# An early activation-table load, five key-weight transfers and a new engine order in a fused attention and gated-MLP kernel

## The chip, the cores and the metric

The kernel runs on one core of one Trainium2 chip. The metric is device time in microseconds (us) of one execution; lower is better. A core has engines that each run their own list of instructions in order and wait for each other by semaphores: TensorE (PE in the profile, with PEld for its weight loads), VectorE (DVE), ScalarE (ACT), GpSimd (POOL) and SyncE (SP). Transfers are issued from SP and ACT and move on 16 DMA engines. Matmul results land in PSUM, everything else lives in SBUF.

## The reference

One transformer block on 2048 tokens of width 640, in bf16. The first half is linear attention with 32 heads of 20 channels, where queries and keys go through a learned feature map (two softmaxes over 20 channels); the second is a bilinear gated MLP of width 1536.

```python
def _A_ref(x, wqkv, w_phi, wo):
    B, S, D = x.shape
    H = 32; Dh = D // H
    q, k, v = ...                                   # x @ wqkv, split in heads
    pq = jnp.einsum("bhsd,hdf->bhsf", q, w_phi)
    pk = jnp.einsum("bhsd,hdf->bhsf", k, w_phi)
    phi_q = concat([softmax(pq), softmax(-pq)], -1)
    phi_k = concat([softmax(pk), softmax(-pk)], -1)
    kv = jnp.einsum("bhsf,bhsd->bhfd", phi_k, v)
    z  = jnp.einsum("bhsf->bhf", phi_k)
    num = jnp.einsum("bhqf,bhfd->bhqd", phi_q, kv)
    den = jnp.einsum("bhqf,bhf->bhq", phi_q, z)[..., None] + 1e-6
    return (num / den).transpose(0, 2, 1, 3).reshape(B, S, D) @ wo

h  = x + _A_ref(_layernorm(x), wqkv, w_phi, wo)
hn = _layernorm(h)
h2 = h + ((hn @ w_gate) * (hn @ w_up)) @ w_down
```

## The kernel before

The 2048 tokens are 16 tiles of 128, the width 640 is 5 chunks of 128. The feature weights are folded into the projections: the product of the key columns of wqkv with a block-diagonal matrix Phi (built from w_phi) is formed once on TensorE, and the same for the queries, so that keys and queries each need one projection per tile. Layer norm is folded in as well: the weights are centred by their column means, and each tile's scale rs multiplies inside the exponential.

**The start.** The steps that the change touches, in the order in which they depend on each other:

- `load_wnat(1, ...)` (L491) brings the key columns of wqkv into Wnat, in chunks of 128 rows (160 KB each). Wnat, and the transposed WT, lie in the memory of the tile phiqT, so the profile calls both phiqT. Before, there are three transfers: chunks 0 and 1 from SP, 2 and 3 from ACT, 4 from SP. w_phi goes into Wrows from ACT, between them. Then SP issues transposing loads of x (`load_xT`, tile xT) and the value columns (tile Wp, 800 KB).
- `warm(32)` (L563) runs 32 matmuls of 128 columns on a constant tile `ones` while the first transfer is under way.
- `wk_in` (L630) takes the key chunks in the order WKC: for each chunk, 5 one-column matmuls for the means and 5 transposes (L639). When the last chunk's means are there, VectorE writes `nmean` (L651). Then the transposed weights are centred and copied out of PSUM in five pieces: pieces 0 and 2 on ScalarE (L658), 1, 3 and 4 on VectorE (L662).
- `wp_round(1, i)` (units x0 to x4, L678) multiplies those pieces with Phi: x0 in three steps (pieces 0 and 1, 2 and 3, then 4), every other round in one step that needs all five. Phi is built on POOL in five pieces (L542). The results are copied into Wp by ScalarE (x0, x2, x4) and VectorE (x1, x3).
- `stats` (units s0, s2, s4, s8, s12, L570) finds mean and scale of 2 or 4 tiles: matmuls on TensorE, copies and sums on VectorE (sm L599, t L604, sxx L607), small operations on POOL (msq L610, vpe, rs L617, nrs L619, mv L621).
- `wv_sums` (unit wv, L711) and `wv_centre` (units c0 to c4, L725) centre the value weights.
- `keys(t)` (units k and K): projection, maximum (L755), bias nb (L758), two exponentials on ScalarE (L762), sums (L773) and reciprocal on VectorE, a product on POOL (L776). `values(t)` (v), `queries(t)` (q and Q, whose results are transposed by DMA into phiqT), `kv_mm` (A0 to A14), `num(t)` (n), `watt(t)` (h: output projection and residual; its result is transposed into hT), `fu` (f, gate and up products) and `fd` (d, e: down product and output) follow.

**The order.** ORDER (L58) is a table with a list of units for each engine: each word stands for the next operation of that unit on that engine. `Prog.place` (L199) walks the lists and assigns buffers; `finish` derives the semaphore waits. So an engine never runs an operation ahead of one that stands before it in its list, and SP issues its transfers in the order of its list: lT4 to lT15 are x transposes, lwq the query columns, t0 to t4 their transposed form, lx0 to lx3 the rows of x for the residual, lwo, lg, lu and ld the weights wo, w_gate, w_up and w_down. PSUM is four buffers (`p_ps`) of two banks. w_down takes the place of the values (tile vaug), so `ld` waits for the last kv_mm.

Of the kernel before, what the change touches and what calls it, by code (L numbers as in the profile page):

```python
# [7 lines left out]
ACT = mybir.ActivationFunctionType  # L8
# [39 lines left out]
WKC = (0, 1, 4, 2, 3)  # L48
# [24 lines left out]
    "DVE":  # L73
# [11 lines left out]
    "ACT":  # L85
# [290 lines left out]
def _build(ctx, nc, A_x, A_wqkv, A_w_phi, A_wo, B_w_gate, B_w_up, B_w_down, out):  # L376
# [5 lines left out]
    def regs(n):  # L382
        return [Reg() for _ in range(n)]
# [669 lines left out]
```

## Time and profile before

| what | value |
|---|---|
| runs | 283.45 us median of 3 (283.38 to 283.68) |
| profiled execution | 283.33 us, of which the span of its instructions is 281.6 us |
| PE busy | 274.1 us, 97% of the span |
| DVE, ACT, POOL busy | 165.9, 133.0, 108.2 us |
| granted TensorE clock | 1.00 over the span |
| chain that ended last, by engine | PE 92%, DVE 3%, ACT 2%, DMA 1%, issue 1% |
| DMA | 28.06 MB, mean 100 GB/s |

Transfers from issue to landing, median us: a 640 KB load of x 5.1, w_up 11.5, w_gate 8.3, w_down 9.3, value columns 5.1; key columns, SP 320 KB 3.9, ACT 320 KB 4.2, SP 160 KB 4.3; w_phi (25 KB) 4.5; a transpose of queries (160 KB) 2.5.

How to read it: an engine's busy time is the union of its instructions' times. The granted clock in the profile starts at its first record, 5.07 us into the span; before that, matmuls of 128 columns start 107 ns apart, and 55 ns after. The chain of waits goes back from the last instruction: at each step to what released it, or to the instruction ahead of it on its engine. A row of the timeline has start, length, engine, line, operation, tiles (out<-in) and count, and in brackets how long the engine had been idle and what ended that.

### The profile page before, as it was taken

The page shows a single profiled execution, that of the slowest core. Times are in us where ns is not written, and L with a number is a line of the kernel's source. Part 1 is how long each engine was busy: PE and PEld are TensorE (multiplying, and loading weights), DVE is VectorE, ACT ScalarE, POOL GpSimd, SP SyncE. Part 2 cuts the span into 40 slices and gives each one's busy share as a digit, 9 for nine tenths or more (in the row PEclk, how much of TensorE's full clock was granted, in tenths as well). Part 3 has the DMA queues.
Part 4 walks back from the last instruction along what each step waited for, and adds up shares of the span by engine and source line. Part 5 has one row for each costly group of instructions (what it writes and reads, how often), then busy time and mean ns, then how long its engine had stood idle before and what let it go on. Part 6 is the DMA issues. An engine that isn't in the chain of part 4 may idle for free.

```text
span 281.6 us, 5487 instructions
## 1 busy us (share of the span) xinstructions
PE 274.1 (97%) x2238; PEld 187.0 (66%) x2251; DVE 165.9 (59%) x289; ACT 133.0 (47%) x225; POOL 108.2 (38%) x160
## 2 busy tenths in 40 slices
PE   8799999999999999999999999999999999999995
PEld 7577778777867888877666554776554444447773
DVE  0699999999989987737756763621402233240211
ACT  0648999799655645226653622023344233330141
POOL 6636889999722522020350354012050051000341
PEclk9999999999999999999999999999999999999999
DMA  7958894018742869925626448164320001000111
GB/s 191 210 120 243 159 262 158 0 38 261 181 85 47 103 137 205 282 48 117 49 48 166 69 94 136 29 140 27 70 72 0 0 0 49 0 0 2 51 72 64
DMA packets 65192, 28.06 MB, mean 100 GB/s; under 512 B 55696, under 2 KB 63888, under 8 KB 65168
## 3 DMA queue, kind: packets, MB, share of 16 engines
q1 hardware_dynamic: 64240, 27.37, 44.2%
q10 hardware_dynamic: 928, 0.35, 0.5%
q8 instruction: 17, 0.28, 0.5%
q14 instruction: 7, 0.06, 0.1%
HBM read 11.82 MB, written 2.62 MB: 51 GB/s over the span
## 4 chain that ended last, share of the span: by engine, by line
PE 92%; DVE 3%; ACT 2%; DMA 1%; issue 1%; POOL 0%; ACTq 0%
PE ps L559 91%; DMA phiqT<-in_A_wqkv_dram 1%; ACT phik L762 1%; DVE ob L874 1%; DVE Wp L725 1%; ACT phiqT L658 1%; ACT L658 0%; DVE phik L916 0%; PE ps L639 0%; PE ps L481 0%; DVE ps L755 0%; DVE outb L957 0%; ACT phik L484 0%; DVE rden L873 0%; DVE Sq L795 0%
## 5 line engine op out<-in xcount | busy, mean ns | idle before, releaser
L559 PE MATMUL ps<-phik,Wgu 128*128 128x512 bf16 (+1 forms) x588 | 105.6, 336 | 0.7
L559 PEld LDWEIGHTS ps<-phik,Wgu 128*128 128x128 bf16 x600 | 58.1, 98 | 43.6 <-DVE phik L916 1.1
L559 PE MATMUL ps<-Wp,xT 128*128 128x320 bf16 x480 | 68.8, 299 | 0.1
L916 DVE TENSOR_TENSOR phik<-ps,gate 128x512 bf16<-128x512 f32 (+1 forms) x60 | 34.0, 580 | 58.1 <-PE ps L559 37.2
L914 ACT ACTIVATE gate<-ps 128x512 bf16<-128x512 f32 (+1 forms) x60 | 29.8, 511 | 74.2 <-PE ps L559 62.7
L559 PE MATMUL ps<-vaug,phik 128*128 128x320 bf16 (+3 forms) x543 | 60.0, 270 | 0.1
L559 PEld LDWEIGHTS ps<-Wp,xT 128*128 128x128 bf16 x480 | 46.2, 98 | 17.9 <-ACT phik L762 0.5
L559 PEld LDWEIGHTS ps<-vaug,phik 128*128 128x128 bf16 x544 | 43.6, 97 | 16.0
L776 POOL TENSOR_TENSOR phik<-phik,Rk 128x1280 bf16<-128x1280 bf16 x16 | 37.5, 2356 | 1.9 <-DVE nb L758 1.4
L932 POOL TENSOR_TENSOR outb<-t,x_all 128x640 bf16<-128x640 f32 x12 | 16.7, 1397 | 54.2 <-ACT t L929 54.1
L801 POOL TENSOR_TENSOR rq<-Sq,rq 128x32 f32<-128x32 f32 x16 | 4.1, 253 | 60.5 <-DVE rq L800 60.5
L755 DVE TENSOR_REDUCE ps<-ps 128x1 f32<-128x640 f32 x32 | 25.8, 812 | 2.3 <-PE ps L559 2.2
L929 ACT ACTIVATE t<-ps,mh,rs 128x640 f32<-128x640 f32 x12 | 10.5, 882 | 34.1 <-PE ps L559 34.1
L795 DVE TENSOR_REDUCE Sq<-eq 128x64 f32<-128x1280 bf16 x16 | 23.6, 1476 | 3.4 <-ACT eq L762 3.3
L773 DVE TENSOR_REDUCE Ssum<-phik 128x64 f32<-128x1280 bf16 x16 | 23.6, 1473 | 0.0
L806 POOL TENSOR_TENSOR eq<-eq,rq 128x640 bf16<-128x640 bf16 x16 | 20.3, 1269 | 1.0
L762 ACT ACTIVATE eq<-ps,nb,rs 128x640 bf16<-128x640 f32 x16 | 14.1, 881 | 8.8 <-DVE nb L758 8.2
L899 POOL TENSOR_SCALAR vpe<-shc 128x1 f32<-128x1 f32 x16 | 3.0, 190 | 38.6 <-ACT junk L552 37.7
L552 ACT ACTIVATE junk<-x_all 128x640 bf16<-128x640 bf16 x20 | 14.8, 741 | 4.9 <-DVE x_all L893 4.9
L762 ACT ACTIVATE phik<-ps,nb,rs 128x640 bf16<-128x640 f32 x16 | 14.3, 893 | 4.0 <-POOL nrs L619 3.3
L782 ACT ACTIVATE vaug<-ps,rs 128x640 bf16<-128x640 f32 x16 | 12.9, 804 | 3.9 <-PE ps L559 3.6
L874 DVE TENSOR_TENSOR ob<-ps,rden 128x640 bf16<-128x640 f32 x16 | 13.0, 814 | 2.4 <-DMA vaug<-ob 2.1
(79 smaller groups left out, 237.1 us busy)
## 6 DMA issues: line engine op xcount, KB each, us to landing
x_all<-in_A_x_dram SPq DMA_DIRECT2D x4, 640.0 KB, 5.1
out_dram<-outb SPq DMA_DIRECT2D x15, 160.0 KB, 1.9
Wgu<-in_B_w_up_dram SPq DMA_DIRECT2D x1, 1920.0 KB, 11.5
Wgu<-in_B_w_gate_dram SPq DMA_DIRECT2D x1, 1920.0 KB, 8.3
vaug<-in_B_w_down_dram SPq DMA_DIRECT2D x1, 1920.0 KB, 9.3
Wp<-in_A_wqkv_dram SPq DMA_DIRECT2D x1, 800.0 KB, 5.1
phiqT<-in_A_wqkv_dram SPq DMA_DIRECT2D x1, 800.0 KB, 6.5
Wo<-in_A_wo_dram SPq DMA_DIRECT2D x1, 800.0 KB, 5.4
```

The source lines that it names most:

```text
L552: g.op("ACT", lambda e: e.activation(out=junk[:, v.i, :], in_=in_, func=func, accum_out=acc), rd=rd, wr=wr, use=[v], t=0.73, lat=0.97)
L559: ins = e.matmul(o_, lhsT=l_, rhs=r_, start=s_, stop=p_, skip_group_check=True)
L755: g.op("DVE", lambda e: e.tensor_reduce(out=mx(), in_=PS[v.i][:, :, 0:HALF], axis=AX.XY, op=ALU.max, apply_absolute_value=True, negate=Tru ...
L762: g.op("ACT", lambda e, s=s, sc=sc: e.activation(out=signed(dst(), s), in_=PS[v.i][:, :, 0:HALF].rearrange("p b (h f) -> p b h f", f=DH), ...
L773: g.op("DVE", lambda e: e.tensor_reduce(out=Ssum[:, vs.i, :], in_=x, axis=AX.X, op=ALU.add), rd=R_phik[t], wr=vs.R, use=[vs], t=1.39, lat=1.5)
L776: g.op("POOL", lambda e: e.tensor_tensor(out=x, in0=x, in1=Rk[:, vr.i, :].unsqueeze(2).to_broadcast([P, 2 * H, DH]), op=ALU.mult), rd=vr.R ...
L795: g.op("DVE", lambda e: e.tensor_reduce(out=Sq[:, vs.i, :], in_=eq[:, b.i, :].rearrange("p (g f) -> p g f", f=DH), axis=AX.X, op=ALU.add), ...
L806: return e.tensor_tensor(out=x, in0=x, in1=rq[:, vr.i, :].unsqueeze(2).to_broadcast([P, H, DH]), op=ALU.mult)
L874: g.op("DVE", lambda e: e.tensor_tensor(out=ob[:, vo.i, :].rearrange("p (b h d) -> p b h d", b=2, d=DH), in0=pv()[:, :, :, 0:DH], in1=rd_( ...
L914: g.op("ACT", lambda e: e.activation(out=gate[:, vg.i, 0:P * n], in_=PS[v.i][:, 0, 0:P * n], func=ACT.Copy), rd=[v.R[0]], wr=vg.R, use=[v, ...
L916: g.op("DVE", lambda e: e.tensor_tensor(out=hhT[:, hb, ft, sl], in0=PS[v.i][:, 1, 0:P * n], in1=gate[:, vg.i, 0:P * n], op=ALU.mult), rd=[ ...
L932: g.op("POOL", lambda e: e.tensor_tensor(out=outb[:, vo.i, :], in0=t32[:, v3.i, :], in1=x_all[:, t, :], op=ALU.add), rd=v3.R + [R_h[t]], w ...
```

## The change

- **Key weights.** Five transfers of one chunk each: SP issues chunks 0, 1 and 3, ACT issues 2 and 4. w_phi is the first transfer of the ACT queue. WKC becomes 0, 1, 2, 3, 4.
- **Table load.** Behind these transfers ScalarE runs an Exp of one column into the scratch tile `junk`, with `ones` as its input. The value columns are then issued from ACT, behind it, where SP issued them before.
- **Phi.** Each of its five pieces has a dependency of its own; the x and y rounds wait for the pieces that they use. (All rounds but x0 use all five.)
- **Warm-up.** 26 matmuls in place of 32.
- **Order.** All five lists of ORDER are new. At the start, x3 and x2 stand ahead of the statistics of s0; POOL's nrs of s0 stands ahead of s2's first operation. On SP, lx2, lx1 and lx0 stand between the first query transposes, lg behind them, and ld directly behind n2's transpose (before: behind Q4's). The planner's figure for a load's rate is 0.38 in place of 0.35; it enters only the choice of buffers and semaphores in `place`.

```diff
-WKC = (0, 1, 4, 2, 3)
+WKC = (0, 1, 2, 3, 4)
...
     "PE":
-        "warm wk wk wk wk wk wk wk wk wk wk s0 x0 s0 x0 x0 x3 x2 x1 x4 wv k0 k0 k0 k0 k0 s2 s2 k1 k3 k2 s4 s4 s4 s4 v3 v1 "
...
+        "warm wk wk wk wk wk wk wk wk wk wk x0 x3 x0 x2 s0 s0 x0 x1 x4 wv k0 k0 k0 k0 k0 s2 s2 k1 k3 k2 v0 s4 s4 s4 s4 k4 "
...
+        "v12 k12 k14 v5 k13 A0 A2 A4 A6 A0 A2 A4 v14 q2 A6 A8 v13 q3 A10 q6 A8 v15 A10 A12 A12 A12 A14 A14 q5 n1 n0 q7 n1 n0 "
+        "n2 h1 h0 h1 q4 n3 h0 h2 f0.7.0 f0.7.0 f0.9.0 f0.9.0 f0.10.0 f0.10.0 f0.11.0 f0.11.0 f0.8.0 f0.8.0 h3 f0.6.0 q8 "
...
     "DVE":
-        "wk wk wk wk s0 s0 x3 s0 x1 c2 c4 k0 s2 s2 k0 c3 s2 k1 c1 k1 c0 k3 k2 s4 s4 k2 s4 k3 K0 s4 K1 K0 k6 K3 k6 k7 K3 "
...
+        "wk wk wk wk x3 s0 s0 s0 x1 c4 c0 k0 s2 s2 k0 c2 k1 c3 k1 c1 s2 k3 k2 K0 s4 k2 s4 s4 k3 s4 k4 K0 K2 k4 K1 k5 K1 "
...
     "ACT":
-        "in in wk wk x0 x4 x2 k0 k0 k1 k1 v3 k3 v1 k3 k2 v7 k2 k6 k6 k7 k7 k5 k5 v2 s12 k4 wm k4 k11 v6 k11 y2 v9 k10 k10 "
...
+        "in in in in in wk wk x2 x0 x4 k0 k0 k1 k1 v0 k2 k2 k3 v2 k3 k4 v3 k4 k5 k5 k7 k7 k6 k6 s12 v9 k10 v10 k10 v7 k9 "
...
     "SP":
-        "in in in in in in in lT6 lT5 lT4 lT7 t1 lT11 lT9 t0 lT8 lT10 lx3 lwq t4 lT14 t2 t3 lT13 lT12 lwo lT15 lu Q0 Q1 "
-        "Q1 lg Q0 lx0 Q2 Q2 Q3 Q3 n2 n3 Q5 Q5 Q7 Q7 h3 h2 Q6 Q6 lx1 n5 n7 Q4 Q4 ld n6 n4 Q8 h7 h6 h4 Q8 Q9 h5 Q9 Q10 Q10 "
...
+        "in in in in in in in lT4 lT6 lT7 lT5 lT8 lT12 lx3 lT9 lT11 lT10 t3 lwq t2 t0 t4 lT14 t1 lwo lT13 lT15 lu Q1 lx2 "
+        "Q1 lx1 Q0 lx0 Q0 lg Q2 Q2 Q3 Q3 n2 ld n3 Q5 Q5 h2 Q7 Q7 h3 Q6 Q6 Q4 n7 Q4 n5 n4 n6 Q8 Q8 Q10 h5 h7 Q10 h4 Q9 h6 "
...
-    load_wnat(1, (0, 2))
-    load_wnat(1, (2, 4), "ACT")
     load(Wrows[:, :, :], A_w_phi.rearrange("h d f -> (h d) f").rearrange("(a p) f -> p a f", p=P), [R_Wrows], 0.03, eng="ACT")
-    load_wnat(1, (4, 5))
-    load_xT(0)
-    load_xT(1)
-    load(Wp[:, :, 2 * D:3 * D], A_wqkv[:, 2 * D:3 * D].rearrange("(c p) n -> p c n", p=P), R_Wp[2], 0.8)
-    load_xT(2)
-    load_xT(3)
+    load_wnat(1, (0, 1))
+    load_wnat(1, (2, 3), "ACT")
+    load_wnat(1, (1, 2))
+    load_wnat(1, (4, 5), "ACT")
+    load_wnat(1, (3, 4))
+    for t in range(4):
+        load_xT(t)
...
+    g.op("ACT", lambda e: e.activation(out=junk[:, 0, 0:1], in_=ones[:, 0:1], func=ACT.Exp), rd=[R_one], wr=[R_tab], t=1.4)
+    load(Wp[:, :, 2 * D:3 * D], A_wqkv[:, 2 * D:3 * D].rearrange("(c p) n -> p c n", p=P), R_Wp[2], 0.8, eng="ACT")
...
-        pool_op(phi_op, 0.4, rd=[R_Wrows, R_G[a]], app=[R_Phi])
+        pool_op(phi_op, 0.4, rd=[R_Wrows, R_G[a]], wr=[R_Phi[a]])
...
-    warm(32)
+    warm(26)
```

More of the change, by code (lines that the diff above doesn't have):

```diff
@@ L448, in _build @@
     R_xT, R_phik, R_vaug = regs(NT), [regs(2) for _ in range(NT)], regs(NT)
-    R_Wnat, R_WT, R_Phi = regs(NC), [regs(NC) for _ in range(2)], Reg()
+    R_Wnat, R_WT, R_Phi = regs(NC), [regs(NC) for _ in range(2)], regs(NC)
     R_Wp = [regs(NC) for _ in range(3)]
@@ L457, in _build @@
     R_mx, R_nb = regs(2 * NT), regs(2 * NT)
-    R_const, R_xone = Reg(), Reg()
+    R_const, R_xone, R_tab = Reg(), Reg(), Reg()
     R_KV, R_Gk = Reg(), Reg()
@@ L463, in load @@
     def load(out_, in_, wr, mb, after=(), eng="SP", app=()):
-        return g.op(eng, lambda e: e.dma_start(out_, in_), wr=wr, app=app, after=after, dma=("w", 8), t=0.6, lat=0.4, size=mb / 0.35)
+        return g.op(eng, lambda e: e.dma_start(out_, in_), wr=wr, app=app, after=after, dma=("w", 8), t=0.6, lat=0.4, size=mb / 0.38)
     def transpose(out_, in_, rd, wr, use=(), t=1.27, size=1.07):
@@ L700, in wp_round @@
             n = len(aa) * (2 - w)
-            g.op("PE", lambda e, lst=lst: mms(e, lst()), rd=[R_WT[w][a] for a in aa] + [R_Phi] + ([R_nmu] if w == 0 else []),
+            g.op("PE", lambda e, lst=lst: mms(e, lst()), rd=[R_WT[w][a] for a in aa] + [R_Phi[a] for a in aa] + ([R_nmu] if w == 0 else []),
                  wr=v.R, use=[v], t=0.062 * n, lat=0.15 + 0.062 * n)
```

73 rows, old and new, of the table ORDER are left out of this document.

## The prediction

> **What bounds the kernel.** I read the page's shares first, then the busy time by stage, then the chain of waits over the first 45 us, and last the order of instructions over the first 16 us. The stages (stretch, length, busy time of PE, PEld, DVE, ACT, POOL):
>
> ```profile
> 0.00:5.00 5.00, 3.83 (x39) 3.58 (x40) 0.00 (x0) 0.00 (x0) 3.54 (x24) 1.00 0.62 169
> 5.00:10.00 5.00, 3.05 (x64) 2.70 (x61) 1.85 (x6) 2.76 (x3) 3.13 (x7) 1.00 1.16 289
> ...
> 20.00:40.00 20.00, 20.00 (x195) 15.21 (x193) 19.67 (x36) 17.10 (x25) 14.72 (x19) 1.00 0.90 204
> 40.00:60.00 20.00, 20.00 (x195) 15.24 (x194) 19.37 (x28) 18.56 (x31) 19.37 (x17) 1.00 0.28 101
> 60.00:80.00 20.00, 20.00 (x279) 16.30 (x278) 18.71 (x33) 15.59 (x29) 16.39 (x12) 1.00 0.62 174
> 80.00:100.00 20.00, 19.34 (x187) 15.26 (x185) 18.69 (x37) 12.53 (x23) 5.48 (x9) 1.00 0.52 79
> ```
>
> From 20 us on TensorE has work without a break; the largest hole is 0.66 us in 80 to 100. None of that work is removed. So the change can win where TensorE waits, before 20 us, or lose by tearing a hole later. VectorE is nearly as full (76.4 of 80 us from 20 to 100), so a hole there costs too. The start, as the chain of waits has it (start, length, what):
>
> ```profile
> 0.79 3.92 DMA phiqT<-in_A_wqkv_dram
> ...
> 4.76 0.30 PE ps L559 x5
> 5.05 0.36 PE ps L639 x5
> 5.41 0.10 PE ps L559 x5
> 5.51 0.30 PE ps L639 x5
> ...
> 6.78 0.18 DVE nmean L651
> ...
> 7.03 1.28 ACT L658
> 8.32 1.49 ACT phiqT L658 x2
> 9.81 0.05 issue
> 9.85 1.65 PE ps L559 x28
> 11.51 0.04 issue
> 11.55 1.53 PE ps L559 x10
> 13.08 0.02 issue
> 13.10 1.55 DVE Wp L725 x2
> ...
> 15.80 0.24 POOL nrs L619
> ```
>
> The reader is to see a strictly serial start: key weights land (4.71), five steps of means and transposes, nmean, then on ScalarE a 1.28 us piece with no tile name, which the order of instructions names:
>
> ```profile
> 1.04 3.59 PE L559 MATMUL ps<-ones 128*128 128x128 bf16 x32 [1.04 <-POOL ones L517]
> 5.91 1.97 POOL L542 TENSOR_TENSOR Phi<-Wrows,G 128x140 bf16<-128x140 bf16 x5 [1.33 <-DMA Wrows<-in_A_w_phi_dram]
> 7.03 1.28 ACT L658 ACT_TABLE_LOAD   x1 [7.03 <-DVE nmean L651]
> 7.08 1.47 DVE L662 TENSOR_SCALAR phiqT<-ps,nmean 128x640 bf16<-128x640 bf16 x3
> ```
>
> **The sum**, against the profiled execution's 283.33 us (span 281.6 and 1.73 around it); the median of the runs, 283.45, is 0.12 higher.
>
> *(a) Key weights and warm-up.* A warm-up matmul costs 0.104 us (3.33 us of weight loads over 32), so 26 end at 1.04 + 2.71, some 3.8, in place of 4.4. Chunk 0 alone (160 KB) is now first on SP, issued at 0.79. No row has a lone 160 KB load from memory at the start: the quick bound is the queries' 160 KB transposes, 2.5 us from issue to landing (3.3), the slow one the 160 KB key chunk that was third in line, 4.3 (5.1). I take 3.0, since it is half of the 320 KB transfer that took 3.92 with nothing ahead: 3.8, just when the warm-up ends. The first step costs 0.65 (0.30 and 0.36 at the slow clock) and the later ones 0.40. Two slow steps, two fast and the last means (0.12): 3.8 + 1.30 + 0.80 + 0.12, and nmean starts at some 6.1 to 6.2, against 6.78. A chunk 0 as late as 4.3 gives the same, because the clock has risen by its second step. The other chunks must keep up. SP issues 1 and 3 at 1.3 and 1.8; ACT issues w_phi, 2 and 4 at 0.8, 1.35 and 1.9 (0.48 to 0.52 each). All key data had landed by 5.60 before; as many bytes on the same engines give 5.3 to 6.3, where the upper end is 4.4 after the last issue. Taken 5.7, under the 6.0 at which chunk 4 has its turn. Term: -0.65, bounds -0.95 and +0.35 (chunk 0 at 5.1 and all five steps after it).
>
> *(b) Table load.* The load (1.28) and a 1-column activation (0.19, the row of L734) now run on ScalarE from 2.4 to 3.9, inside its idle time up to 7.03: cost nothing there. From nmean's start to the last centred piece took 3.03 (6.78 to 9.81); without the load VectorE's three pieces end 1.77 after it (8.55) and ScalarE's two 1.74 (0.25 + 1.49). Term: -1.26. The value weights queue behind it on ACT: issued at 3.9, landed at 9.0 by the 5.09 us that this transfer took before, needed at 10.2. The cover is 1.2 us; a transfer of over 6.3 us would show.
>
> *(c) Order of the start.* The two statistics groups of s0 (0.28 each) filled the wait before; now they stand behind x3 and x2, which need all five pieces, so they lie on the path: +0.57. PSUM has four buffers and each x round finds one free in this order. The value sums then start at 11.55 - 0.65 - 1.26 + 0.57 = 10.2.
>
> *(d) nrs.* POOL's negated scale of s0 stood behind s2's first operation and came at 16.03, when the key bias was ready at 15.85; now it stands ahead of it. Term -0.1 (bounds -0.2 and 0).
>
> w_phi first and one dependency per Phi piece: VectorE and ScalarE have all pieces at 7.9; even a w_phi landing as late as before gives Phi at 7.88. Nothing; if Phi came later, x3 would wait for it one for one.
>
> *(e) The rest of the order.* On SP the value load (0.58) leaves and a third key chunk (0.45) comes, so the x transposes start 0.5 later and end as before; the last of the four that s8 needs should land at 25, needed at 27; the last query weight transpose at 34 to 35, needed near 40. x_all 1 and 2 and w_gate move to 58 to 66 us, and 3.8 MB at the rate of w_gate's 1.9 MB in 8.3 us are in by 76, before the next query transposes (75.9 before). w_down moves from 108 to just behind n2's transpose, at 84.6 - 1.35 = 83.3, and n3's transpose is queued behind it: w_down landed after 9.26, so 92.6, and the transpose 0.6 later (the trace's gap at 117.4 to 118.0): 93.2, against h3's turn at 94.40 - 1.35 = 93.05. Taken +0.1 for all. Bounds: -0.66 (the hole of 80 to 100 closed) and +2.4 (w_down as slow as w_up, below).
>
> Sum: -0.65 - 1.26 + 0.57 - 0.1 + 0.1 = -1.34, so 282.0 us.
>
> By the Trainium skill (DMA: Bandwidth & Descriptors, "Issuing engines are not separate DMA queues") all queues share the same 16 engines and a second one saves only issue time. The rows lean that way: four first transfers of 25 to 320 KB took 3.9 to 4.5 us whatever their size; by the rule (a) is near nothing and the time is the first rival's.
>
> **The rivals.**
> *Splitting brings nothing (0.20).* The 1.1 us from the issue to the first packet in the trace and a slow first flow set the landing, and chunk 0 comes at 4.7. For it: 25 KB took 4.5 us, 320 KB 3.9. Against it: the 25 KB and the 160 KB stood behind others. nmean at 6.78, the other terms stay: 283.33 - 0.69 = 282.6.
> *The gain is lost behind the start, or the table is loaded twice (0.11).* VectorE at 96% from 20 to 100 lets a worse fit of order give back 1.2 us, or the early Exp brings a table set that Identity does not find, and 1.28 comes back at the old place. Against the latter: one load serves Identity, Exp, Square and Copy in the whole trace. About 283.2.
> *w_down too early (0.11), slower.* If w_down takes the 11.5 us of w_up (same size) and not 9.26, n3's transpose lands at 83.3 + 11.5 + 0.6 = 95.4 and TensorE, in order, stands before h3 for 2.35 us: 282.0 - 0.1 + 2.35 = 284.2. It turns the sign from a landing of 94.5 on. For it: transposes share those engines in that stretch; against it: w_up stood behind w_o and a transpose, w_gate took 8.3.
> *The clock stays low (0.08), slower.* The 32 warm-ups ran at 107 ns apart, the transposes at 55 only from 5.1 on. With 26 and gaps between landings TensorE may stay slow to the value sums: steps of 0.65 put nmean at 6.75, and 2.2 us of x rounds and statistics double: 282.0 + 0.6 + 2.2 = 284.8. It turns the sign when the slow clock lasts beyond some 10 us (0.6 and 0.75 of doubled work). Against it: the gaps are short.
> The Trainium skill (TensorE: Matmul & The Clock Gate, Part 1) counts some 3.4 us of sustained work in a free-running window; 26 warm-ups are 2.7 us, so by it the matmuls behind them have to fill in. The trace agrees on about 4 us before the rise (1.04 to 5.1).
>
> **How the numbers follow.** The forecast has 0.50, the rivals 0.20, 0.11, 0.11 and 0.08. A measurement tells 0.2%, some 0.57 us, from no change, so faster means under 282.88. Forecast (nearly whole) and three quarters of the first rival: 0.64; a quarter of it, most of the second and a little of the forecast: 0.15; the last two and a tail of the second: 0.21. Low end 281.3: (a) at -0.95 and half of the hole of 80 to 100 closed. High end 283.9: it takes in the first rival, chunk 0 at its slow bound (283.0) and the second rival with half a us of (e) on top, and leaves out most of the last two.
>
> **What would show it.** Right: the table load at 2.4 with nothing waiting for it; nmean at 5.9 to 6.4; x3 at 7.7 to 8.2; the value sums at 10.0 to 10.5; ScalarE's first Exp at 14.4 to 14.8; PE over 19.9 of 20 us in each stretch from 20 to 80. Wrong: nmean at 6.7 or later (a), a second table load (b), value sums that wait for a DMA (b), 128-column matmuls 107 ns apart after 6 us, or an idle TensorE ahead of h3 near 93 us (e).

## The result and the profile after

The changed kernel takes 285.35 us in the median of 22 runs (284.40 to 286.92), against 284.33 us for the kernel before in 22 runs on the same chip: ratio 1.0036, 95% interval 1.0019 to 1.0053, so it is slower by about a third of a per cent. The forecast was 282.0, with 283.9 as the high end. The profiled execution took 285.47 us, its span 283.7.

The busy time by stage of the changed kernel (stretch, length, busy time of PE, PEld, DVE, ACT, POOL with counts, granted clock, DMA share, GB/s):

```profile
0.00:5.00 5.00, 3.96 (x50) 3.96 (x51) 0.00 (x0) 1.49 (x2) 3.96 (x26) 1.00 0.63 162
5.00:10.00 5.00, 2.58 (x40) 1.81 (x38) 1.63 (x4) 1.48 (x2) 3.05 (x7) 0.80 1.21 228
10.00:15.00 5.00, 5.00 (x42) 4.31 (x41) 2.47 (x5) 2.11 (x3) 2.20 (x6) 0.52 0.94 142
15.00:20.00 5.00, 5.00 (x44) 3.67 (x42) 4.42 (x9) 1.64 (x2) 0.64 (x3) 1.00 0.62 117
20.00:40.00 20.00, 20.00 (x172) 14.86 (x171) 19.81 (x38) 16.84 (x24) 13.48 (x22) 1.00 1.02 214
...
60.00:80.00 20.00, 20.00 (x265) 16.12 (x263) 19.18 (x33) 16.88 (x29) 18.20 (x15) 1.00 0.84 226
80.00:100.00 20.00, 19.54 (x192) 15.30 (x191) 17.54 (x36) 11.73 (x23) 4.37 (x8) 1.00 0.96 195
```

From 20 us on this is as full as before; the stretch from 80 to 100 is even a little fuller (19.54, before 19.34). The difference stands in the second and third rows: 2.58 us of work where there were 3.05, and then 5.00 us of busy TensorE at a granted clock of 0.52. Before, the clock was 1.00 in every row. The chain of waits over the start (start, length, what):

```profile
1.28 0.55 ACTq L464
...
1.85 5.38 DMA phiqT<-in_A_wqkv_dram
...
7.28 0.28 PE ps L560 x5
7.56 0.32 PE ps L640 x5
...
7.90 1.49 ACT phiqT L659 x2
9.38 0.08 issue
9.47 35.53 PE ps L560 x330
```

Before, the first transfer held the chain to 4.71. Now the last chunk does (chunk 4, the second key transfer of ACT's queue), to 7.24. The table load is gone from between nmean and ScalarE's pieces. From 9.47 on it is TensorE alone. The order of instructions at the start (start, length, engine, line, operation, tiles, count, and in brackets how long the engine had been idle and what ended that):

```profile
2.34 1.28 ACT L517 ACT_TABLE_LOAD   x1 [2.34 <-issue]
2.40 0.40 ACTq L464 DMA_DIRECT2D Wp<-in_A_wqkv_dram  x1
...
6.38 0.28 PE L560 MATMUL ps<-ones,phiqT 128*128 128x1 bf16 x5 [0.91 <-DMA phiqT<-in_A_wqkv_dram]
...
7.28 0.28 PE L560 MATMUL ps<-ones,phiqT 128*128 128x1 bf16 x5 [0.32 <-DMA phiqT<-in_A_wqkv_dram]
...
13.27 2.27 PE L560 MATMUL ps<-Wp,ones 128*128 128x320 bf16 x10
```

Three things are to be seen. The value load went out at 2.40, while the table load in front of it ran from 2.34 to 3.62: on ACT the issue of a transfer does not wait for the instruction ahead of it to end. TensorE stood for chunk 3 and again for chunk 4. And the value load took 8.3 us from issue to landing where it had taken 5.1, as the DMA issues of the first 20 us have it, first before, then after (transfer, queue, count, KB, us to landing):

```profile
Wp<-in_A_wqkv_dram SPq DMA_DIRECT2D x1, 800.0 KB, 5.1
```

```profile
Wp<-in_A_wqkv_dram ACTq DMA_DIRECT2D x1, 800.0 KB, 8.3
```

The x transposes in flight beside it took 8.49 and 7.67 us, before 4.68 and 3.86.

The clock records give 1.0 from 4.55, 0.5 from 7.97 and 1.0 again from 14.79; here are the two stretches between them:

```profile
4.55:7.97 3.42, 2.08 (x42) 1.56 (x39) 0.24 (x2) 0.07 (x1) 3.42 (x11) 1.00 1.08 213
7.97:14.79 6.82, 5.74 (x46) 4.88 (x47) 3.86 (x8) 3.51 (x5) 2.11 (x7) 0.50 1.07 177
```

The slow stretch is 6.82 us, twice 3.41, and it came after a stretch of 3.41 us in which TensorE was busy for 2.08. The matmuls in it start twice as far apart: the first six of the value sums 267 ns, before 135. The last four start behind the rise, and all ten take 2.27 us, before 1.53.

The two profiled executions, step by step (us):

| from ... to | before | after | difference |
|---|---|---|---|
| start to nmean on VectorE | 6.78 | 7.60 | +0.82 |
| to the rest of the x rounds | 3.07 | 1.87 | -1.20 |
| to the value sums | 1.70 | 3.80 | +2.10 (0.57 of it put down to the two statistics groups, at the 0.28 each that they took before; 1.53 to the clock) |
| to the first key projection | 1.35 | 2.11 | +0.76 (the clock) |
| to the end of the span | 268.70 | 268.32 | -0.38 |
| sum | 281.60 | 283.70 | +2.10 |

This sum is larger than the 1.0 us between the medians, because the kernel before also loses clock in some executions: in 35 of them beside the first experiments, the 19 under 283.9 us have a mean granted clock of 0.999 or 1.0, and 15 of the 16 above 284.6 us have 0.993 or 0.994, which is one window of 3.41 us at half clock. Of the changed kernel's 22 executions ten have 0.987 or 0.988 (two such windows, the profiled one among them) and five 0.993 or 0.994. The other seven have 0.999 or 1.0 and still take 284.71 to 286.92 us, 285.03 in the median. A mean of 1.0 does not show that the clock was up early, since no record is made before the first rise (e4 below), and these seven have no trace. So the table holds for the profiled execution; how much of the loss between the medians is the clock's is not shown.

### The profile page after: what moved, and what is told of

It reads as the page before. It is cut to its first block, busy times and chain, and to the rows that moved or that the text cites. A ratio compares the mean times of both kernels' runs of the same rounds, so it can differ in the third digit from the quotient of the medians.

```text
span 283.7 us, 5474 instructions
## 1 busy us (share of the span) xinstructions
PE 276.1 (97%) x2231; PEld 188.8 (67%) x2245; DVE 165.6 (58%) x289; ACT 133.8 (47%) x226; POOL 108.2 (38%) x160
## 4 chain that ended last, share of the span: by engine, by line
PE 95%; DMA 2%; ACT 1%; issue 0%; DVE 0%; ACTq 0%
PE ps L560 95%; DMA phiqT<-in_A_wqkv_dram 2%; ACT phiqT L659 1%; DVE outb L958 0%; ACTq L464 0%; PE ps L481 0%; ACT phik L484 0%; PE ps L640 0%
## 5 line engine op out<-in xcount | busy, mean ns | idle before, releaser
L894 DVE SCALAR_TENSOR_TENSOR x_all<-ps,mh,x_all 128x640 bf16<-128x640 f32 x16 | 14.0, 880 | 0.5
```

The source lines that it names most:

```text
L894: g.op("DVE", lambda e: e.scalar_tensor_tensor(out=xv, in0=PS[v.i][:, :, 0:HALF], scalar=mh[:, t:t + 1], in1=xv, op0=ALU.subtract, op1=ALU ...
```

## The experiments

The theory formed from this: the value load on ACT's queue, in flight beside the transposing loads of x on SP's queue, slows both and the key chunks with them; TensorE then waits, and the waits cost it the clock. The rivals: the value load is merely too early; five small transfers are late by themselves; the loss is in the new order or in the 26 warm-ups. All warm-up and filler matmuls below multiply a constant tile and nothing uses their results. A median is given with the ratio to the kernel before on the same chip and its 95% interval. The ratio is the figure to compare: the median of the kernel before moved between 283.59 and 284.77 from set to set, and the ratio is not the quotient of two medians.

### The first four: one part each

**e1**, the changed kernel with the value load back on SP:

```diff
-load(Wp[:, :, 2 * D:3 * D], ..., eng="ACT")
 load_xT(0); load_xT(1)
+load(Wp[:, :, 2 * D:3 * D], ...)
```

> The changed kernel, but the value load (800 KB) goes back to SP behind the x transposes of tiles 0 and 1, where it stood before. Theory 'contention' (the value load, issued on ACT at 2.4 us while the table load ran, shares the DMA engines with key chunks 3 and 4 and holds them up): chunk 4 lands by 5.8 in place of 7.24, nmean starts at 6.0 to 6.4 in place of 7.60, the first keys projection starts at 11.3 to 11.8 in place of 15.38, and the kernel takes about 282.0 us, 1.3 less than before. Theory 'clock' (26 warm-ups and short bursts leave TensorE's clock low whatever the transfers do): nmean comes early too, but matmuls of 128 columns are still 107 ns apart between 8 and 11 us, the first projection starts later than 13, and the time is not below that of before. Theory 'order' (the new order loses after the start): the first projection is 1.2 us earlier than before, but the span is not shorter.

283.45 us, ratio 0.9978 (0.9950 to 1.0005), where the changed kernel has 1.0036: 0.58% of some 284 us, or 1.6 us, gone by moving one transfer. The value load took 5.6 us from issue to landing, in place of 8.3; the first x transpose landed at 7.04 (10.67 with the load on ACT), chunk 4 at 6.39 (7.24). But nmean came only at 6.91, and the clock still fell:

```profile
5.00:10.00 5.00, 3.50 (x56) 2.99 (x57) 2.06 (x5) 1.48 (x2) 3.07 (x7) 0.82 1.22 265
10.00:15.00 5.00, 5.00 (x51) 4.24 (x49) 3.33 (x7) 2.11 (x3) 2.44 (x7) 0.83 0.96 142
```

That is the busy time by stage of e1; the column before the last two is the clock, 0.82 and 0.83: one slow window, where the changed kernel had two. So the queue is one part of the loss; the late chunks and the clock are what is left here.

**e2**, the kernel before with the early one-column Exp and nothing else:

```diff
+g.op("ACT", lambda e: e.activation(out=junk[:, 0, 0:1], in_=ones[:, 0:1], func=ACT.Exp), rd=[R_one], wr=[R_tab], t=1.4)
```

> The kernel before with nothing but the early one-column Exp (ScalarE's table load ahead of nmean). Theories 'contention' and 'order': nmean at 6.8 as before, the five centred pieces done at 8.55 in place of 9.81, the first projection 1.2 us earlier (11.7), and a time of 1.0 to 1.3 us less than before, since nothing else changed. Theory 'clock': the idle stretch of TensorE ahead of the x rounds gets shorter (1.85 to some 0.6 us), so its clock holds at least as well as before; a gain under 0.5 us would mean that the 1.28 us were hidden behind something that no view shows.

282.54 us, ratio 0.9947 (0.9924 to 0.9970). This part of the change brings what was forecast for it. The chain of waits of e2:

```profile
7.44 1.49 ACT phiqT L659 x2
...
8.97 1.65 PE ps L560 x28
...
10.66 1.53 PE ps L560 x10
```

ScalarE's pieces stand directly behind nmean (7.14 here), and the rest of the x rounds starts 1.83 us after it, where it took 3.07.

**e3**, the changed kernel with filler matmuls where TensorE waits for the chunks and for the centred pieces:

```diff
-warm(26)
+for n_ in (26, 10, 8, 16, 10): warm(n_)
```

> The changed kernel, with 10, 8, 16 and 10 further 128-column matmuls on the constant tile in TensorE's waits (ahead of key chunks 3 and 4, ahead of the first x round and behind its first step); transfers untouched. Theory 'clock': the clock stays at 1.0 from its rise on, the 28 matmuls of the x rounds take 1.65 us and the value sums 1.36, so the first projection starts at 12.6 to 13.2 in place of 15.38 and the kernel gains about 2 us on the changed kernel (283.0 to 283.5, about the time of before). Theory 'contention': nmean stays at 7.4 to 7.8, because fillers move no transfer; so the kernel does not get below 283. If the clock falls all the same, or the time stays at 285, the clock is not what the 2 us hang on.

284.81 us, ratio 1.0024 (0.9996 to 1.0051), a miss. The clock did as the theory says: up at 4.70 and never down, and the first projection at 13.25 (15.38 in the changed kernel), though the value load still landed at 10.19. Not all of that is the clock's: chunk 4, whose transfer is the same, landed at 6.46 in this execution (7.24 there), and nmean came at 7.05 where 7.4 to 7.8 was expected. So the 7.24 is one execution's, and that the value load holds up the key chunks is not shown. The time followed only in part: 4.2 us from numerators to output projection became 5.3 (78.23 to 83.55). The order of instructions of e3 shows two holes of TensorE that the changed kernel's profile does not have:

```profile
83.16 0.55 PE L560 MATMUL ps<-KVsb,phiqT 128*128 128x84 bf16 x10 [1.51 <-DMA phiqT<-eq]
...
96.20 1.54 PE L560 MATMUL ps<-Wo,phik 128*128 128x320 bf16 x10 [0.50 <-DMA phik<-ob]
```

The first is n2, which waits for a query transpose that landed at 83.07, behind w_gate on SP (issued 70.44, landed 81.79); the second is h3, which waits for n3's transpose (96.15), behind w_down (86.24 to 95.69). Both loads stand there by the new list of SP. In the changed kernel's profile w_gate landed just as late, at 82.13, but the query transpose for n2 landed at 83.41 and n3's at 95.90, and TensorE, some 2 us later from the start on, came to n2 at 83.99 and to h3 at 96.50: 0.6 us behind each.

**e4**, the changed kernel with the three key transfers of before, and the value load on SP:

```diff
-WKC = (0, 1, 2, 3, 4)
+WKC = (0, 1, 4, 2, 3)
...
+    load_wnat(1, (0, 2))
+    load_wnat(1, (2, 4), "ACT")
     load(Wrows[:, :, :], ..., eng="ACT")
+    load_wnat(1, (4, 5))
```

> The changed kernel with all loads of the start as before (three key transfers, w_phi second on ACT, chunk order 0 1 4 2 3, the value load on SP); the early table load, 26 warm-ups and the new order stay. Theory 'contention': key chunks land as before (4.7 to 5.6), nmean at 6.8, and the x rounds at 8.6 behind it; with the two statistics groups on the path the value sums start at 10.8 to 11.0 and the time is about 0.6 us below before (282.6 to 282.9). Theory 'clock': with 26 warm-ups TensorE is idle from 3.8 to 4.7 and the clock rises a window (3.4 us) later or falls in the wait; then the first projection is at 13 or later and the time is that of before or above. Against the first kernel of this set it shows what splitting the key load is worth with the value load out of its way.

284.82 us (282.01 to 286.44), ratio 1.0009 (0.9976 to 1.0042). All chunks were there at 5.52, yet nmean came at 7.64. The order of instructions shows why:

```profile
4.64 0.29 PE L560 MATMUL ps<-ones,phiqT 128*128 128x1 bf16 x5 [0.64 <-DMA phiqT<-in_A_wqkv_dram]
...
7.46 0.69 PE L640 MATMUL ps<-ident,phiqT 128*128 128x128 bf16 x5
...
13.56 2.48 PE L560 MATMUL ps<-Wp,ones 128*128 128x320 bf16 x10
```

The 26 warm-ups ended 0.64 us before the first chunk, five transposes still took 0.69 us at 7.46 (0.44 at the full clock), and the first clock record is a rise at 15.50. The page's mean clock of 1.00 says nothing of this, as no record is made before the first rise. The profiled execution is the slowest of the twelve, at 286.44 us, and the fastest took 282.01, so not all of them need have been so; but the forecast's rival of a clock that stays low is real, in this kernel.

### Chunks, warm-ups and fillers

**e5**, five chunks again, all on SP in their order, w_phi alone on ACT:

```diff
+for c in range(NC): load_wnat(1, (c, c + 1))     # SP; the value load on SP behind load_xT(1)
```

> The changed kernel with all five key chunks issued on SP, one after the other, ahead of the x transposes; ACT issues w_phi alone, and the value load is on SP behind tiles 0 and 1. So no transpose is in flight beside a load of the other queue. Theory 'mixing' (x transposes on SP's queue beside key chunks on ACT's hold both up: in the first experiment packets of both stood still for up to 1 us until 5.97, and chunk 4 landed at 6.39): chunk 0 lands at 3.2 as with two queues, chunk 4 by 5.4, with 0.3 between its first and last engine, and nmean starts by 6.2 in place of 6.91. Rival 'five small transfers are slow by themselves' (each pays a fixed time): chunk 4 lands at 6.2 or later, nmean at 6.8. Whether the clock holds decides the time: 282.0 if it does, 283.5 if not.

282.64 us, ratio 0.9940 (0.9917 to 0.9963). The chunks landed at 3.25, 3.97, 5.35, 5.76 and 6.21. That chunk 4 is late because it shares ACT's queue falls: alone on SP the fifth is nearly as late as in e1 (6.39). Three transfers of the same bytes were in by 5.5 to 5.8 in all profiles that have them. Five small ones are later here, and nmean (7.01) gains nothing by the early chunk 0.

**e6**, e2 with fillers that bridge TensorE's wait between the transposes and the x rounds:

```diff
-warm(32)
+warm(34)
...
+g.op("PE", lambda e: mms(e, [(PS[vs[2].i][:, 1, P:2 * P], ones[:, :], ones[:, :], True, True) for _ in range(15)]), ...)
```

> The kernel before with the early one-column Exp, two more warm-ups (34) and 15 further matmuls on the constant tile between the first statistics group and the first x round; loads and order otherwise as before. Theory 'clock' (the two groups of times, 282.0 to 282.7 and 283.1 to 283.7 with the table load alone, come from where the free window of the clock falls on TensorE's waits): the upper group is gone or nearly so, 10 of 12 runs lie under 282.8 and the median is 282.1 to 282.3. Rival 'the groups have another cause' (transfers, the chip): still a third or more of the runs above 283.

282.44 us (281.92 to 283.30), ratio 0.9934 (0.9913 to 0.9955): the lowest median of all kernels here, and faster than the kernel before and the changed one; the intervals of e2 and e5 overlap its own. The order of instructions of e6:

```profile
6.79 0.45 PE L560 MATMUL ps<-xT 128*128 128x129 bf16 x5
7.08 1.00 PE L560 MATMUL ps<-ones 128*128 128x128 bf16 x15
...
8.53 1.65 PE L560 MATMUL ps<-Phi,phiqT 128*128 128x80 bf16 x28
10.22 1.52 PE L560 MATMUL ps<-Wp,ones 128*128 128x320 bf16 x10
11.57 1.52 PE L560 MATMUL ps<-Wp,xT 128*128 128x320 bf16 x10
```

The fillers (7.08 to 8.08) cover most of the wait for the pieces and lie in nobody's way; the first projection starts at 11.57, before at 12.90. All twelve executions have a mean clock of 1.0, and eleven are under 282.8 us, where e2 has seven of twelve from 282.0 to 282.66 and five from 283.05 to 283.71. That e2's upper five had a late clock is not shown: their means are 1.0 too, and the trace kept is of one of the seven.

**e8**, e4 with 32 warm-ups:

```diff
-warm(26)
+warm(32)
```

> The kernel with three key loads and the value load on SP (early table load and new order), now with 32 warm-ups in place of 26 and nothing else. With 26 its profiled execution had the clock rise only at 15.5 us and its median was 284.8. Theory 'clock' (the 0.9 us of idle TensorE between 3.8 and 4.7 keep a window from counting as busy): the clock rises by 6.5 us in most runs, the median falls by 1 us or more, to 282.6 to 283.6. Rival 'the warm-ups do not matter, the new order's idle stretch ahead of the x rounds does': the median stays above 284.

283.31 us, ratio 0.9960 (0.9936 to 0.9983), against e4's 1.0009: some 1.4 us. The clock rose at 4.33, and its order of instructions has the same transposes and value sums as e4 at the full clock:

```profile
6.74 0.44 PE L640 MATMUL ps<-ident,phiqT 128*128 128x128 bf16 x5
...
10.95 1.52 PE L560 MATMUL ps<-Wp,ones 128*128 128x320 bf16 x10
```

**e9**, the order of before with e6's table load and fillers, 26 warm-ups, five chunks on SP and w_phi alone on ACT:

```diff
-warm(34)
+warm(26)
...
+for c in range(NC): load_wnat(1, (c, c + 1))     # SP
```

> The order of before, with the early table load, five key chunks on SP in the order 0 to 4, w_phi alone on ACT, 26 warm-ups and 15 fillers ahead of the first x round. If both 'mixing' and 'clock' hold: nmean at 6.0 to 6.2, the first projection at 11.2 to 11.5 (12.02 with the table load alone), times around 281.5. If small transfers are slow by themselves: nmean at 6.7 or later and a time as with the table load alone (282.5).

283.00 us, ratio 0.9963 (0.9941 to 0.9985). nmean 6.67, as in e6 (6.69), so five chunks bring nothing over three here either; they push the value load to a landing at 10.83, and the value sums wait for it.

### What the chunks and the order are worth

**e10**, e5 with w_phi moved behind the chunks on SP:

```diff
-load(Wrows, ..., eng="ACT")
 for c in range(NC): load_wnat(1, (c, c + 1))
+load(Wrows, ...)
```

> The kernel with five key chunks on SP, with w_phi moved from ACT to SP behind chunk 4; nothing else differs. Theory 'w_phi first' (its 640 packets of 40 bytes, moved at 2.3 to 3.2 us amid chunks 0 to 2, are why chunk 2 landed at 5.35 and chunk 4 at 6.21): chunk 4 lands at 5.2 to 5.6 and nmean starts by 6.4. Rival 'five transfers are slow by themselves': chunk 4 stays at 6.0 to 6.4, nmean at 6.8 to 7.0, time 282.6 as before within 0.4.

283.17 us, ratio 0.9977 (0.9957 to 0.9998). Chunk 4 landed at 5.80, between what the two theories gave: w_phi ahead of the chunks accounts for about 0.4 of its delay, and what is left is at the edge of the 5.5 to 5.8 of the three transfers. nmean was at 6.44, the earliest of all. But w_phi now landed at 6.41, the x rounds waited 0.71 us for Phi, the clock fell again (9.06 to 12.47) and the first projection came at 13.60.

**e11**, e2 with the value load on ACT behind the Exp; the order of before, three key transfers, 32 warm-ups:

```diff
-load(Wp[:, :, 2 * D:3 * D], ...)
+load(Wp[:, :, 2 * D:3 * D], ..., eng="ACT")
```

> The kernel before with the early table load, and the value load moved to ACT behind it (issued at 1.9 to 2.4 us); three key loads, 32 warm-ups and the order of before stay. Theory 'contention' (the early value load by itself costs the gain): the x transposes of tiles 0 and 1 land at 9 to 11 in place of 6.4 and 7.0, so the first statistics group holds TensorE ahead of the x rounds, the first keys projection starts at 13.5 or later (12.02 with the table load alone), and the median is 284 or more against 282.54. Rival (the value load only hurts chunks that come after it, and with three key loads there are none): key chunks land by 5.7, projection at 12.0 to 12.4, median 282.3 to 282.9.

286.61 us, ratio 1.0097 (1.0067 to 1.0127), against e2's 0.9947: 1.5% or some 4 us, by moving one transfer. The DMA issues in the first 20 us (transfer, queue, count, KB each, us from issue to landing), first of e2, then of e11:

```profile
Wp<-in_A_wqkv_dram SPq DMA_DIRECT2D x1, 800.0 KB, 5.0
```

```profile
Wp<-in_A_wqkv_dram ACTq DMA_DIRECT2D x1, 800.0 KB, 9.1
```

The first x transpose took 9.44 us beside it. TensorE stood for that, as e11's order of instructions has it:

```profile
11.29 0.72 PE L560 MATMUL ps<-xT 128*128 128x129 bf16 x5 [3.57 <-DMA xT<-in_A_x_dram]
```

and the clock was at half from 10.02 to 16.85. So this one line costs e2 more than the changed kernel loses, without the new order and without five chunks. The wait is another one, though: here the statistics of s0 stand ahead of the x rounds, where in the changed kernel they stand behind x3 and x2 and its profile shows no such wait; what the load costs there is e1's 1.6 us.

**e12**, e8 with 34 warm-ups and 18 fillers ahead of x0, so the new order with three key transfers:

```diff
-warm(32)
+warm(34)
...
-"warm wk wk wk wk wk wk wk wk wk wk x0 x3 ..."
+"warm wk wk wk wk wk wk wk wk wk wk wk x0 x3 ..."
...
+g.op("PE", lambda e: mms(e, [(PS[vs[2].i][:, 1, P:2 * P], ones[:, :], ones[:, :], True, True) for _ in range(18)]), ...)
```

> The new order with the early table load, three key loads, the value load on SP, 34 warm-ups and 18 fillers on TensorE ahead of the first x round. Against the same start with the order of before (282.44) it shows what the new order is worth when the clock holds. Theory 'clock': the spread of the times shrinks, 10 of 12 under 283 (32 warm-ups without fillers: 282.06 to 284.12). Theory 'order': if the two statistics groups behind x3 and x2 cost their 0.57 us and nothing later pays it back, the median is 282.9 to 283.1; if the rest of the new order is 0.4 better, as the profiled executions say, 282.4 to 282.6.

283.32 us (282.49 to 284.41), ratio 0.9968 (0.9946 to 0.9990). Against e6, which differs in the order, in Phi's dependencies by piece and in three fillers: the first projection is 0.54 later (12.11 and 11.57; nmean 6.72 and 6.69), which is the two statistics groups, and from there to the end of the span it takes 0.52 longer (269.16 and 268.64). One hole in its order of instructions has that size, and e6 has no wait of TensorE for a transfer after 20 us:

```profile
94.39 1.54 PE L560 MATMUL ps<-Wo,phik 128*128 128x320 bf16 x10 [0.53 <-DMA phik<-ob]
```

This is h3, waiting for n3's transpose (landed 94.34) behind w_down (84.40 to 93.75): the prediction's rival of w_down too early. With the clock up from 4.08 in the profile the spread still did not shrink as expected: 3 of 12 are under 283 us.

**e13**, e5 with 18 fillers ahead of x0:

```diff
+g.op("PE", lambda e: mms(e, [(PS[vs[2].i][:, 1, P:2 * P], ones[:, :], ones[:, :], True, True) for _ in range(18)]), ...)
```

> The new order with five key chunks on SP (w_phi first on ACT, value load on SP, 26 warm-ups) and 18 fillers ahead of the first x round. Theory 'clock': the runs at 283.0 to 284.1 without fillers go, median 282.2 to 282.5. Theory 'splitting brings nothing': it lies within 0.3 of the kernel with three key loads and fillers of this set, since nmean starts at 6.7 to 7.0 in both.

282.64 us, ratio 0.9971 (0.9949 to 0.9993; this chip's median of before is 283.59, e5's was 284.65). nmean 6.74, first projection 12.26, near e5's 12.40: beside e5 the fillers show no gain in the median, and the 282.2 to 282.5 of the clock theory was missed. Two executions still took 283.95 and 284.44 us at a mean clock of 1.0.

### Too early, or the other queue?

**e14**, the changed kernel, where the value load waits for the Exp:

```diff
-load(Wp[:, :, 2 * D:3 * D], ..., eng="ACT")
+g.op("ACT", lambda e: e.dma_start(Wp[:, :, 2 * D:3 * D], ...), rd=[R_tab], wr=R_Wp[2], ...)
```

> The changed kernel with one wait more: ACT issues the value load only when the one-column Exp has ended, at some 3.9 us, which is where the prediction had put it, in place of 2.40. Theory 'early' (the 1.5 us by which the issue ran ahead of the table load are what hurts): chunk 4 lands by 6.4 as with the value load on SP, and the median falls to 283.5. Theory 'other queue' (a large load on ACT's queue beside x transposes on SP's slows both, whenever it is issued): the transposes of tiles 0 and 1 still land at 9.5 to 11.5 and the value load takes 7 us or more; median 284.8 to 285.6, about the changed kernel's.

287.56 us, ratio 1.0109 (1.0059 to 1.0158). The issue moved from 2.40 to 3.86, chunk 4 (6.08), nmean (6.60) and the first x transpose (7.66) are early now. But the load lands at 13.44 and the second x transpose at 13.09, 9.55 after its issue, so the value sums start at 14.96 and the first projection is at 16.83. A load of 7 us or more is what the theory of the other queue expects; of the two transposes one came earlier and one later than its 9.5 to 11.5, and the median is some 2 us above its 284.8 to 285.6. Its DMA issue:

```profile
Wp<-in_A_wqkv_dram ACTq DMA_DIRECT2D x1, 800.0 KB, 9.6
```

**e15**, e11 with the value load held back until the second x transpose has landed:

```diff
-load(Wp[:, :, 2 * D:3 * D], ..., eng="ACT")
+g.op("ACT", lambda e: e.dma_start(Wp[:, :, 2 * D:3 * D], ...), rd=[R_xT[1]], wr=R_Wp[2], ...)
```

> The order of before with the early table load and three key loads, and the value load on ACT, issued only when the x transpose of tile 1 has landed (about 7.0 us); the transposes of tiles 2 to 5 are then under way on SP. Theory 'other queue': key chunks and tiles 0 and 1 land as before (5.6, 6.4, 7.0), the value load takes 7 us or more from issue to landing (5.0 on SP) and lands at 14 or later, and tiles 2 and 3 land later than 10.8; value sums at 14 or later, median above 285. Theory 'early': away from the key chunks the value load takes its 5.0 us, lands at 12, tiles 2 and 3 land by 11; value sums at 12.2, some 1.5 later than with the table load alone, and the median is 283.7 to 284.2.

288.15 us, ratio 1.0104 (1.0051 to 1.0156). The key weights (5.66), nmean (6.83) and both first x transposes (6.53 and 7.12) are unharmed. The load, issued at 7.14, still takes 7.8 us, the transpose issued next to it at 7.10 takes 7.99, and the value sums wait (order of instructions):

```profile
14.97 2.31 PE L561 MATMUL ps<-Wp,ones 128*128 128x320 bf16 x8 [4.14 <-DMA Wp<-in_A_wqkv_dram]
```

Issued at 1.91, 2.40, 3.86 or 7.14 us, this load takes 7.8 to 9.6 us on ACT's queue; issued on SP's, 5.0 to 5.6 (at 4.47 before, 4.85 in e1). "Too early" falls, "the other queue" stands. No run has this load on ACT's queue with no transposes in flight on SP's; before, the 320 KB key load took 4.24 us on ACT's queue and 3.92 on SP's, so a load on ACT's queue is not so much slower by itself.

## Why the prediction was wrong

- **(b), the table load, was right in mechanism and size.** One load, at 2.34, with nothing waiting for it; from nmean to the rest of the x rounds -1.20 against the -1.26 forecast; alone (e2) it makes the kernel 0.5% faster.
- **(b), the value load, is the step that failed.** The prediction put it as "issued at 3.9, landed at 9.0 by the 5.09 us that this transfer took before". The issue was at 2.40 and the landing at 10.71. The error is not the issue, which was 1.5 us earlier than forecast, but the duration, taken from the same transfer on another queue. On ACT's queue, with x transposes in flight on SP's, it took 8.3, and the first transpose, 4.68 before, took 8.49. The cover of 1.2 us was worked out for the value sums alone; that the load would slow the transposes was not in the sum. Moving it back is worth 1.6 us (e1); moving it in the kernel before with the early table load costs some 4 us (e11). By which wait it costs the changed kernel its 1.6 us is open: in its profile TensorE is late for key chunks and by the clock, and shows no wait for the load or an x transpose. In e3, where the clock held, TensorE waited 0.38 us for one.
- **(a), key weights, failed too.** Chunk 0 came even earlier (3.28) than the 3.8 taken, but nmean hangs on the last chunk: 7.24, against 5.7 taken and 6.3 as the upper end from "as many bytes on the same engines". In the other profiles the last of five is at 5.8 to 6.5, with the value load on ACT's queue too (6.46 in e3, 6.08 in e14), so the upper end of that bound was nearly right and the value to take. The rival that splitting brings nothing was the better forecast: nmean at 6.4 to 7.0 with five chunks in e1, e5, e9, e10 and e13, 6.7 to 6.9 with three in the kernel before, e6, e8, e12 and e15 (7.1 to 7.6 in e2, e4 and e11, where the clock rose only at 6.25 us or later). The terms of the prediction's sum for nmean add up to 6.02, not to the 6.1 to 6.2 that it goes on with. The Trainium skill (DMA: Bandwidth & Descriptors, "Issuing engines are not separate DMA queues") says that a second issuing engine saves only the time of issue; the chunks agree (the last at 6.39 from two engines in e1, at 6.21 from one in e5), while the value load shows that it can also cost 4 us.
- **The rival of the low clock named the right resource with another cause.** It took 26 warm-ups as too few for the rise, and gave 284.8 us a chance of 0.08. The rise came in time, at 4.55. The clock was lost after it, when TensorE had waited for chunks and pieces, and this made +2.29 us (1.53 + 0.76) of the profiled execution, its largest term. It is not the same share of the median: e3 holds the clock and gains 0.5 us. What the rival described did happen in e4. The prediction's list of signs held it: matmuls 107 ns apart after 6 us.
- **(c)** forecast +0.57. The changed kernel's profile cannot tell it from the clock, as the groups ran at half clock there; with the clock up, e12 against e6 has +0.54.
- **(d) and (e)**: after the first projection the changed kernel is 0.38 us faster, against 0.0 for the two terms together. That is in part luck. The sum had w_gate in by 76, ahead of the next query transposes; it was issued only at 72.44 and landed at 82.13, and TensorE passed the transposes behind w_gate and w_down with 0.6 us to spare. Profiles of the same order with another start do wait for a query transpose, 1.51 us in e3, 1.18 in e4, 1.11 in e10 and 0.27 in e13, and 0.50 and 0.53 ahead of h3 in e3 and e12. So the rival of w_down too early is real, at about a fifth of its price, and the wait behind w_gate, put at nothing, too. A gain lost to VectorE is not seen in the changed kernel. The hole of 0.66 us in 80 to 100, which the lower bound of (e) closes, is two holes in the trace, 0.41 and 0.23.
- **The sum:** -1.34 forecast. Had (a) been nothing and the clock kept, -1.20 + 0.57 - 0.38 leave -1.0, about what e13 shows, which has the value load on SP as well (282.64 against 283.59).

Open stay: what slows a load on ACT's queue beside transposes on SP's; why the changed kernel's executions without a recorded slow window are hardly faster; and what 32 warm-ups, or w_gate and w_down at their old places, would do in the changed kernel itself, which was not tried.

## What to carry to other kernels

Before a transfer is moved to another engine's queue, look at what is in flight on the first: its old duration doesn't go with it, and the transfers that it now runs beside pay as well. Where TensorE waits in the first microseconds behind its warm-up, unused matmuls in the wait can hold the clock. In e6 they did so at no cost; in e3 and e13 the median gained little or nothing. Where a start gets faster, look again at the transfers further on: a load that was early enough for a late TensorE can hold up an early one (e3, e12). When one serial piece can be taken off the path by itself, measure it alone before anything is built around it: here that one line makes the kernel 0.5% faster, and the whole change makes it 0.4% slower.

## What the runs showed of the hardware

- A plain load of 800 KB takes 5.0 to 5.6 us on SP's queue, among the x transposes, and 7.8 to 9.6 us on ACT's queue beside them; transposes beside it take up to 9.55 (up to 6.81 with the load on SP's queue, in e6). The two do not merely share busy engines: with both under way in e11, the 16 engines moved 125, 36 and 24 GB/s in the three half microseconds from 7.0 to 8.5 us, where e2 moved 364, 364 and 380. What holds them is not shown.
- ACT issues a transfer while the table load ahead of it still runs (2.40 within 2.34 to 3.62); a dependency on the Exp held it back in e14 (3.86).
- The clock fell without an idle window. The Trainium skill (TensorE: Matmul & The Clock Gate, Part 1) has the clock return to half after at least one idle window of about 3.4 us. Here the length agrees (3.41 us), but TensorE was busy for 2.08 of it, and in e1 for 2.16. In e5 it was busy for 2.10 of the window behind the rise and the clock stayed up, so busy time alone does not give the bound.
- Six warm-ups, some 0.6 us, were worth some 1.4 us in the ratios of e4 and e8. In the profiled executions the clock stayed low to 15.5 us with 26 warm-ups that end 0.64 us before the first data (e4, its slowest execution), and rose at 4.33 with 32 (e8).
